# A long-convolution and GLU kernel on one core: six PSUM banks for the transforms and two for the GLU, with a new written order

## The chip, the core and the metric

The kernel runs on one core of a Trainium2 chip. TensorE multiplies matrices and writes its results to PSUM, which has eight banks of 2 KB in each of 128 partitions. VectorE (DVE) and ScalarE (ACT) read PSUM and SBUF. SyncE (SP) issues almost all DMAs here, in one queue. The metric is the time of one execution in device microseconds (us); lower is better. A profile of one execution, taken on the chip, gives the start and duration of every instruction and who waited for whom.

## The reference

Two branches work on the layer-normalised input and are added to it. All tensors are bf16; S is 2048, D is 640, F is 1728.

```python
x = A_q
xn = layernorm(x)                                    # over D
# branch A: a causal convolution over the whole sequence
k_shift = sum over t in 0..3 of k delayed by t, times shift_k[:, t]
kv = k_shift * v
y = irfft(rfft(kv, 2S) * rfft(ssm_k, 2S))[:S]        # per channel, along S
A = xn * (y + kv * ssm_D)
# branch B: a gated linear unit
B = (sigmoid(xn @ w_gate) * (xn @ w_up)) @ w_down
out = x + A + B
```

## The kernel before

The kernel interleaves the two branches on TensorE.

**Branch B** goes in four passes (`tr` 0 to 3) of 512 tokens. A pass transposes its normalised tokens to `xnT` (by TensorE for the first two passes in `rec_tp`, L700; by a transposing DMA for the others, L694). Then it goes through 14 chunks of 128 of F (`rec_fc`, L752): five matmuls for the gate and five for the up projection (L764), each into a PSUM bank of its own; a sigmoid of the gate on ACT (L728 or L722); and a multiply of sigmoid and up on VectorE into `hT` (L730), or, for some chunks, a copy of up to SBUF first (L316) and a multiply from there (L725). The last chunk holds gate and up in one bank. The first two chunks of the first pass are computed in pieces of 128 tokens as they arrive (`rec_first`, L735, matmuls L744). At the end of a pass `rec_down` (L771) projects each of its four 128-token tiles back to 640 columns: 14 chunks for each of two column halves of 320 (L782), and VectorE adds each half to the accumulator `acc` (L794).

**Branch A** treats the 640 channels as two halves of five sub-blocks, ten in all. For each sub-block VectorE makes `kv` from `k` and `v` (`rec_kv`, L468 to L484, eight operations), and TensorE goes through three transform stages: `rec_st1` (L503, once for the kernel spectrum and once for `kv`), `rec_st2` (L523, four groups) and, after a complex product on VectorE (`rec_prod`, L553 and L556, or L547 where a DMA swaps the halves), `rec_st3` (L575 and L577, two groups). Each group of matmuls fills one pair of PSUM banks (stage 1 fills two pairs) and is evacuated by a copy of 1024 elements per partition on ACT (L316, L319) or VectorE (L317, L320). After five sub-blocks `rec_st4` (L607) finishes a half. Stages 1, 2 and 4 use parts of the array (32 or 64 rows); stage 3, the GLU and the down projections use all of it. Before all of that come the fix-up of `k`'s first rows (`load_kv`, L426, with its evacuation L317 or L316) and the shift filter's broadcast (L389).

**What sets the order.** Every operation is recorded with what it reads and writes, and then issued in the order of a written-out list, `ORDER` (L80); the cost figures passed to `pe`, `act` and `dve` and the priorities don't take part in that. An operation that ACT or VectorE could do goes to VectorE if it is in `ON_DVE` (L124). Each engine and SP's queue work in that order. Buffers come from pools named in `SLOTS` (L279): `"c"` are pairs of PSUM banks (two, so four banks), for the transforms, the shift and fix-up matmuls and the first pass's transposes; `"g"` are single banks (four) for GLU and down projections, the second pass's transposes and a warm-up. Where an operation takes a buffer, it gets, among those whose users have all been issued, the one used least recently; on the chip it then waits until those users are done.

The statistics of a token tile (L641 sums, L647 squares) run on ACT, in two batches: tiles 4 to 7 in the first pass, 8 to 15 around the first down projections. Normalised tokens are also written to DRAM (L687).

Of the kernel before, what the change touches and what calls it, by code (L numbers as in the profile page):

```python
# [21 lines left out]
P = 128  # L22
# [20 lines left out]
def _dft_tables():  # L43
# [37 lines left out]
    6, 0, 5, 1, 4, 2, 8, 7, 3, 11, 10, 13, 12, 9, 14, 16, 71, 72, 15, 73, 74, 75, 91, 17, 86, 76, 96, 77, 104, 97,  # L81
    78, 571, 81, 79, 87, 88, 82, 80, 83, 92, 89, 84, 90, 148, 85, 94, 93, 572, 98, 100, 99, 102, 101, 149, 103, 589,
    42, 150, 151, 152, 155, 153, 57, 154, 157, 563, 156, 158, 564, 64, 565, 590, 567, 566, 568, 569, 62, 573, 570,
    18, 61, 574, 575, 63, 577, 58, 576, 578, 579, 56, 581, 580, 582, 59, 583, 585, 107, 584, 106, 586, 607, 587, 108,
    591, 588, 66, 105, 592, 593, 608, 109, 110, 595, 594, 19, 111, 609, 596, 113, 43, 68, 597, 599, 60, 112, 598, 29,
    600, 601, 114, 603, 65, 604, 605, 602, 610, 67, 606, 611, 612, 39, 614, 613, 44, 615, 45, 133, 134, 20, 136, 616,
    617, 23, 619, 135, 618, 27, 620, 621, 116, 623, 31, 622, 625, 624, 118, 626, 115, 32, 627, 41, 120, 628, 119, 40,
    631, 122, 25, 629, 632, 121, 630, 35, 117, 633, 123, 634, 126, 637, 128, 635, 30, 636, 130, 638, 127, 639, 131,
    26, 640, 129, 37, 643, 642, 125, 641, 649, 124, 650, 132, 24, 651, 38, 653, 644, 655, 652, 21, 654, 162, 22, 69,
    645, 656, 646, 657, 658, 36, 647, 648, 33, 659, 660, 34, 163, 662, 95, 164, 165, 663, 664, 172, 167, 667, 665,  # L90
    137, 28, 661, 159, 666, 669, 166, 668, 161, 168, 47, 671, 160, 670, 50, 169, 672, 673, 48, 171, 143, 170, 46,
    178, 674, 144, 52, 173, 676, 180, 54, 179, 677, 138, 49, 174, 678, 51, 181, 175, 139, 680, 53, 675, 183, 182,
    290, 681, 682, 70, 176, 140, 195, 186, 685, 683, 141, 295, 196, 294, 199, 142, 177, 201, 200, 185, 686, 184, 202,
    145, 197, 293, 187, 689, 296, 198, 679, 291, 188, 687, 690, 292, 203, 297, 204, 192, 692, 189, 694, 205, 193,
    206, 695, 194, 207, 190, 209, 208, 191, 227, 210, 217, 228, 216, 233, 146, 234, 219, 211, 147, 218, 231, 220,
    212, 688, 232, 221, 229, 698, 298, 55, 230, 222, 684, 691, 223, 213, 696, 235, 699, 214, 249, 703, 236, 215, 237,
    701, 224, 238, 248, 704, 226, 240, 251, 225, 243, 239, 250, 259, 244, 697, 735, 260, 253, 265, 736, 693, 707,
    700, 252, 705, 266, 241, 755, 706, 711, 242, 702, 254, 261, 708, 263, 255, 262, 712, 280, 709, 264, 713, 267,
    245, 268, 717, 281, 246, 247, 714, 269, 718, 270, 283, 256, 715, 716, 719, 271, 257, 258, 723, 282, 272, 273,
    310, 274, 710, 720, 311, 275, 722, 721, 314, 276, 729, 315, 316, 299, 286, 312, 317, 730, 288, 313, 731, 318,  # L100
    277, 319, 287, 724, 278, 320, 732, 279, 321, 284, 322, 725, 285, 391, 734, 307, 301, 395, 300, 726, 309, 733,
    756, 737, 333, 308, 302, 324, 727, 739, 728, 394, 342, 323, 325, 738, 304, 397, 343, 303, 396, 344, 740, 346,
    392, 305, 345, 393, 332, 741, 347, 348, 743, 326, 349, 289, 742, 327, 350, 351, 746, 744, 374, 352, 367, 745,
    328, 748, 354, 747, 330, 329, 750, 353, 306, 388, 752, 775, 355, 751, 390, 331, 757, 749, 389, 334, 753, 358,
    336, 759, 356, 335, 359, 398, 754, 758, 337, 357, 338, 761, 760, 400, 368, 763, 401, 762, 399, 403, 369, 404,
    764, 766, 765, 371, 370, 767, 768, 372, 375, 769, 776, 770, 373, 381, 376, 772, 795, 771, 378, 797, 377, 777,
    773, 379, 339, 830, 779, 774, 380, 778, 341, 340, 360, 781, 402, 382, 783, 780, 782, 405, 406, 383, 784, 407,
    786, 384, 433, 385, 432, 411, 788, 785, 787, 435, 412, 386, 417, 436, 415, 418, 387, 790, 416, 413, 792, 789,
    791, 414, 796, 798, 419, 793, 420, 794, 361, 800, 362, 799, 363, 364, 365, 802, 801, 806, 803, 805, 422, 421,
    408, 424, 807, 423, 409, 434, 808, 410, 804, 425, 437, 366, 443, 426, 812, 438, 444, 439, 449, 465, 427, 450,  # L110
    464, 813, 467, 428, 468, 445, 447, 446, 809, 448, 814, 831, 810, 429, 811, 451, 815, 430, 431, 452, 818, 817,
# [10 lines left out]
    940, 941, 913, 923, 943, 947, 914, 946, 915, 945, 944, 917, 916, 936, 938, 939, 937  # L122
]
ON_DVE = [  # L124
    45, 133, 135, 620, 622, 34, 144, 179, 183, 141, 196, 145, 146, 266, 247, 258, 315, 329, 773, 340, 416, 364, 448,
    431, 463, 474, 500, 480, 478, 502, 495, 498, 490, 514, 534, 545, 546, 888, 553, 559
]

# [91 lines left out]
def kernel(  # L220
# [107 lines left out]
    def mm(n):  # L328
        return n / 2.4 + 3.0
# [405 lines left out]
    def rec_first(pri):  # L735
# [13 lines left out]
        for fc in range(2):  # L749
            rec_evac(0, fc, cs[fc], gt())  # L750
# [173 lines left out]
```

## Time and profile before

| | us |
|---|---|
| median of 10 runs (lowest to highest) | 270.58 (269.28 to 271.89) |
| profiled execution | 270.83 |
| span in its profile | 269.1 |
| TensorE busy | 256.4 |
| VectorE busy | 189.3 |
| ScalarE busy | 158.2 |
| GLU matmuls (L764), 520 of 128x512 | 121.1 busy |
| down matmuls (L782), 448 of 128x320 | 67.0 busy |

The span is from the first to the last instruction in the profile; the rest of the execution's time lies around it. Matmuls overlap, so the mean duration of one (380 ns for L764) is longer than the distance between two starts (216 ns), and "busy" says little of what is lost. The kernel has one stream of work on TensorE, so what costs time is a stretch in which TensorE works on nothing, or at a lower clock, and the question for each is what it waited for. The page gives the clock that TensorE was granted in tenths of full speed, for 40 slices of 6.7 us.

### The profile page before, as it was taken

The page shows a single profiled execution, that of the slowest core. Times are in us where ns is not written, and L with a number is a line of the kernel's source. Part 1 is how long each engine was busy: PE and PEld are TensorE (multiplying, and loading weights), DVE is VectorE, ACT ScalarE, POOL GpSimd, SP SyncE. Part 2 cuts the span into 40 slices and gives each one's busy share as a digit, 9 for nine tenths or more (in the row PEclk, how much of TensorE's full clock was granted, in tenths as well). Part 3 has the DMA queues.
Part 4 walks back from the last instruction along what each step waited for, and adds up shares of the span by engine and source line. Part 5 has one row for each costly group of instructions (what it writes and reads, how often), then busy time and mean ns, then how long its engine had stood idle before and what let it go on. Part 6 is the DMA issues. An engine that isn't in the chain of part 4 may idle for free.

```text
span 269.1 us, 9709 instructions
## 1 busy us (share of the span) xinstructions
PE 256.4 (95%) x4375; PEld 156.1 (58%) x4375; DVE 189.3 (70%) x329; ACT 158.2 (59%) x235; POOL 0.7 (0%) x6
## 2 busy tenths in 40 slices
PE   8899988999999797999999999999999999999992
PEld 3754435755445555777655546577676466545771
DVE  4433376256999999876979969698776846558541
ACT  3844949962887696646788456556366666422200
POOL 1000000000000000000000000000000000000000
PEclk9999997999999999999999999999999999999998
DMA  6999899999946191999976163371354647400761
GB/s 176 330 327 316 158 216 149 148 138 303 131 104 152 40 298 61 148 158 154 192 148 170 44 185 90 80 174 31 82 146 148 178 94 217 118 2 5 178 178 40
DMA packets 90448, 40.40 MB, mean 150 GB/s; under 512 B 66592, under 2 KB 88040, under 8 KB 90088
## 3 DMA queue, kind: packets, MB, share of 16 engines
q1 hardware_dynamic: 90216, 39.47, 66.8%
q8 instruction: 34, 0.56, 0.9%
q10 hardware_dynamic: 192, 0.33, 0.4%
q14 instruction: 6, 0.05, 0.1%
HBM read 30.61 MB, written 5.24 MB: 133 GB/s over the span
## 4 chain that ended last, share of the span: by engine, by line
PE 76%; DVE 14%; DMA 3%; SPq 2%; ACT 2%; issue 1%; ACTq 1%; DVEq 0%
PE g L764 33%; PE g L782 23%; PE c L523 6%; PE c L607 4%; PE c L575 3%; PE c L577 3%; PE c L503 2%; DVE P L553 2%; DVE ta L473 2%; DVE tb L468 1%; SPq L445 1%; DMA acc<-in_A_q_dram 1%; PE g L744 1%; DMA ht<-in_A_ssm_k_dram 1%; DVE S L556 1%; DVE xq L678 1%
## 5 line engine op out<-in xcount | busy, mean ns | idle before, releaser
L764 PE MATMUL g<-xnT,w 128*128 128x512 bf16 x380 | 89.6, 380 | 0.0
L782 PE MATMUL g<-wd,hT 128*128 128x320 bf16 x448 | 67.0, 304 | 0.0
L764 PEld LDWEIGHTS <-w 128*128 128x128 bf16 x380 | 34.0, 98 | 36.5
L782 PEld LDWEIGHTS <-hT 128*128 128x128 bf16 x448 | 42.8, 99 | 17.8
L730 DVE TENSOR_TENSOR hT<-sig,g 128x512 bf16<-128x512 bf16 x34 | 23.1, 686 | 19.5 <-PE g L764 12.9
L316 ACT CAST S<-c 128x1024 bf16<-128x1024 f32 x31 | 30.8, 1017 | 8.6 <-PE c L523 8.5
L728 ACT ACTIVATE sig<-g 128x512 bf16<-128x512 f32 x34 | 20.2, 596 | 20.0 <-PE g L764 16.9
L764 PE MATMUL g<-xnT,V 128*128 128x512 bf16 x140 | 31.5, 380 | 0.0
L523 PEld LDWEIGHTS <-Mt 64*128 64x128 f16 x1280 | 20.4, 95 | 10.2 <-issue 9.5
L794 DVE TENSOR_TENSOR acc<-g,acc 128x320 bf16<-128x320 f32 x32 | 14.4, 486 | 16.3 <-PE g L782 16.3
L523 PE MATMUL c<-T,Mt 64*128 64x64 bf16 x1280 | 23.9, 191 | 1.7 <-ACT V L316 1.6
L316 ACT CAST V<-c 128x1024 bf16<-128x1024 f32 x17 | 17.0, 1014 | 10.2 <-PE c L577 10.2
L764 PEld LDWEIGHTS <-V 128*128 128x128 bf16 x140 | 13.4, 98 | 15.2
L575 PE MATMUL c<-At,S 128*128 128x128 f16 x160 | 19.8, 220 | 2.2 <-DVE S L556 1.9
L722 ACT ACTIVATE sig<-g 128x512 bf16<-128x512 f32 x18 | 10.8, 602 | 16.5 <-PE g L764 16.2
L316 ACT CAST T<-c 128x1024 bf16<-128x1024 f32 x15 | 14.7, 1015 | 9.6 <-PE c L503 9.4
L577 PE MATMUL c<-At,P 128*128 128x128 f16 x160 | 19.6, 219 | 0.0
L575 PEld LDWEIGHTS <-S 128*128 128x128 bf16 x160 | 15.5, 98 | 4.4 <-DVE S L556 3.6
L319 ACT ACTIVATE T<-c 128x1024 bf16<-128x1024 f32 x14 | 13.9, 1024 | 5.6 <-PE c L503 5.6
L553 DVE TENSOR_TENSOR P<-S 64x1024 bf16<-64x1024 bf16 x20 | 13.7, 685 | 4.6 <-ACT S L316 4.2
L577 PEld LDWEIGHTS <-P 128*128 128x128 bf16 x160 | 15.6, 98 | 1.2 <-issue 0.7
L317 DVE CAST S<-c 128x1024 bf16<-128x1024 f32 x9 | 11.0, 1224 | 4.3 <-PE c L523 4.3
(84 smaller groups left out, 264.5 us busy)
## 6 DMA issues: line engine op xcount, KB each, us to landing
w<-in_B_w_gate_dram SPq DMA_DIRECT2D x7, 640.0 KB, 5.7
w<-in_B_w_up_dram SPq DMA_DIRECT2D x7, 640.0 KB, 5.3
kt<-in_A_k_dram SPq DMA_DIRECT2D x8, 320.0 KB, 7.8
vt<-in_A_v_dram SPq DMA_DIRECT2D x8, 320.0 KB, 5.5
xnd<-xq SPq DMA_DIRECT2D x4, 640.0 KB, 5.2
P<-S SPq DMA_DIRECT2D x10, 256.0 KB, 3.9
ht<-in_A_ssm_k_dram SPq DMA_DIRECT2D x16, 96.0 KB, 4.3
wd<-in_B_w_down_dram SPq DMA_DIRECT2D x3, 480.0 KB, 9.1
```

The costliest lines, as they stand in the source:

```text
L316: fa = lambda: nc.scalar.copy(out=out_fn(), in_=in_fn())
L317: fd = lambda: nc.vector.tensor_copy(out_fn(), in_fn())
L319: fa = lambda: nc.scalar.activation(out_fn(), in_fn(), ACT.Copy, scale=scale)
L523: nc.tensor.matmul(tl[c][:, b, 64 * kk:64 * kk + 64], lhsT=Mb[rows, k, 64 - 64 * r:192 - 64 * r], rhs=tl[T][rows, 2 * k + r].rearrange("p ...
L553: dve(n, 2, lambda a=a, o=o, b=b: nc.vector.tensor_tensor(Q(b)[a], X(b)[a], H(b)[o], ALU.mult), r=sr + ([(Z, b, 1)] if h else []), w=[(Z, ...
L575: nc.tensor.matmul(o, lhsT=tl[S_][:, b, 0, j, :], rhs=Ab[:, 2 if zc else 0, :], start=True, stop=zc)
L577: nc.tensor.matmul(o, lhsT=tl[Z][:, b, j, :], rhs=Ab[:, 1, :], start=False, stop=True)
L728: act(512, lambda: nc.scalar.activation(tl[sg][:], tl[cs[0]][:], ACT.Sigmoid), r=[(cs[0],)], w=[(sg,)], alloc=[(sg, "sig")], pri=pri - 2000)
L730: dve(512, 1, lambda: nc.vector.tensor_tensor(hT[:, fc, :], tl[sg][:], tl[cs[1]][:], ALU.mult), r=[(cs[1],), (sg,)], w=[(hk, fc)], pri=pri ...
L764: nc.tensor.matmul(tl[c][:], lhsT=w()[:, k, o:o + P], rhs=tl[X][:, k, :], start=(k == 0), stop=(k == NC - 1))
L782: nc.tensor.matmul(tl[pd[i]][:, 0:320], lhsT=hT[:, fc, t4 * P:(t4 + 1) * P], rhs=wd[:, fc, 320 * i:320 * i + 320], start=(fc == 0), stop=( ...
L794: dve(320, 1, lambda i=i, m=m, pd=pd: nc.vector.tensor_tensor(acc[:, m, 320 * i:320 * i + 320], tl[pd[i]][:, 0:320], acc[:, m, 320 * i:320 ...
```

## The change

- `SLOTS`: `"c"` has three pairs of banks, and `"g"` two banks; still eight in all.
- `rec_first` and `rec_evac`: the first two chunks of the first pass, gate and up, now go to a pair of banks each from `"c"` (`c0_0`, `c0_1`), not to four banks from `"g"`.
- `rec_down`: every token tile is computed as the last one was before: first column half (chunks 0 to 6, then 7 to 13), then the other half, where a tile's two halves went chunk by chunk together. A half takes its bank when it begins.
- The key `"last"` puts the down projection of token tile 15 behind that of tile 14; before, tile 15 came first and tile 14 ended the kernel.
- `ORDER` and `ON_DVE` are new lists. The shift matmul (operations 42 to 45) comes earlier and so do the copies of `M` (40, 41); the `k` multiplies begin during the first pass's down projections; `ON_DVE` has 30 entries, before 40.
- The cost figures in `pe`, `MG` and `MD` are changed.

```diff
 ORDER = [
...
 ]
 ON_DVE = [
-    45, 133, 135, 620, 622, 34, 144, 179, 183, 141, 196, 145, 146, 266, 247, 258, 315, 329, 773, 340, 416, 364, 448,
-    431, 463, 474, 500, 480, 478, 502, 495, 498, 490, 514, 534, 545, 546, 888, 553, 559
+    45, 136, 135, 622, 34, 160, 182, 141, 140, 145, 202, 215, 210, 264, 313, 308, 330, 285, 371, 378, 384, 431, 450,
+    480, 495, 497, 504, 520, 545, 560
 ]
...
-             "ta": 1, "tb": 1, "T": 2, "S": 2, "P2": 1, "V": 1, "c": 2, "g": 4}
+             "ta": 1, "tb": 1, "T": 2, "S": 2, "P2": 1, "V": 1, "c": 3, "g": 2}
...
     def rec_evac(tr, fc, cs, pri):
+        two = isinstance(cs, str)
+        pk = lambda i: (cs, i) if two else (cs[i],)
+        pv = lambda i: tl[cs][:, i] if two else tl[cs[i]][:]
...
-            act(512, lambda: nc.scalar.activation(tl[sg][:], tl[cs[0]][:], ACT.Sigmoid),
-                r=[(cs[0],)], w=[(sg,)], alloc=[(sg, "sig")], pri=pri - 2000)
-            dve(512, 1, lambda: nc.vector.tensor_tensor(hT[:, fc, :], tl[sg][:], tl[cs[1]][:], ALU.mult),
-                r=[(cs[1],), (sg,)], w=[(hk, fc)], pri=pri - 2000)
+            act(512, lambda: nc.scalar.activation(tl[sg][:], pv(0), ACT.Sigmoid),
+                r=[pk(0)], w=[(sg,)], alloc=[(sg, "sig")], pri=pri - 2000)
+            dve(512, 1, lambda: nc.vector.tensor_tensor(hT[:, fc, :], tl[sg][:], pv(1), ALU.mult),
+                r=[pk(1), (sg,)], w=[(hk, fc)], pri=pri - 2000)
...
     def rec_first(pri):
-        cs = [[f"pg0_{fc}_{u}" for u in range(2)] for fc in range(2)]
-        every = [(cs[fc][u], fc, u) for fc in range(2) for u in range(2)]
+        every = [(fc, u) for fc in range(2) for u in range(2)]
...
-                            nc.tensor.matmul(tl[c][:, i * P:(i + 1) * P], lhsT=weight(0, u)[1]()[:, k, o:o + P],
+                            nc.tensor.matmul(tl[f"c0_{fc}"][:, u, i * P:(i + 1) * P], lhsT=weight(0, u)[1]()[:, k, o:o + P],
...
-                   alloc=[(c, "g") for c, _, _ in grp] if i == 0 else (), pri=FIX + 1)
+                   alloc=[(f"c0_{fc}", "c") for fc in range(2)] if i == 0 else (), pri=FIX + 1)
...
         for t4 in range(4):
...
-            last = m == NQ - 1
-            parts = ([(0, 7, (0,)), (7, 14, (0,)), (0, 7, (1,)), (7, 14, (1,))] if last else
-                     [(c0, c1, (0, 1)) for c0, c1 in ((0, 4), (4, 8), (8, 11), (11, 14))])
+            parts = [(0, 7, (0,)), (7, 14, (0,)), (0, 7, (1,)), (7, 14, (1,))]
...
-                          ([("z",)] if c1 == 14 else []) + ([("cv", u) for u in range(4)] if m >= PRM["ML"] and c0 == 0 else []),
-                          w=[(pd[i],) for i in ii], pri=gt())
+                          ([("z",)] if c1 == 14 else []) + ([("cv", u) for u in range(4)] if m >= PRM["ML"] and c0 == 0 else []) + ([("last",)] if m == NQ - 1 and c0 == 0 else []),
+                          w=[(pd[i],) for i in ii] + ([("last",)] if m == NQ - 2 and c1 == 14 else []), pri=gt())
```

## The prediction

> **What bounds the kernel now.** I read the page's busy shares first, then its slices, the stages by window, and last the chain and the single queues.
>
> ```profile
> PE 256.4 (95%) x4375; PEld 156.1 (58%) x4375; DVE 189.3 (70%) x329; ACT 158.2 (59%) x235; POOL 0.7 (0%) x6
> ...
> PEclk9999997999999999999999999999999999999998
> ```
>
> TensorE is the bound over the whole span, but "busy" covers lost time, so I ask where. One clock digit is a 7, in the slice 40.4 to 47.1 us. The stages by window (columns: stretch, length, busy time of PE, weight loads, DVE, ACT, POOL, clock, DMA share, GB/s):
>
> ```profile
> 38.00:47.00 9.00, 7.26 (x50) 4.41 (x48) 5.81 (x9) 7.68 (x16) 0.00 (x0) 0.81 1.19 174
> 80.00:104.00 24.00, 20.61 (x447) 12.71 (x446) 23.65 (x40) 17.50 (x21) 0.00 (x0) 1.00 0.56 158
> ```
>
> From 80 to 104 us VectorE is busy for 23.65 of 24 us: here it sets the pace, not TensorE. From 38 to 47 us the clock was 0.81. The timeline of that stretch:
>
> ```profile
> 38.97 0.43 PE L389 MATMUL c<-xq,Ft 128*128 128x320 bf16 x2
> ...
> 40.68 0.73 PE L700 MATMUL g<-ident,xq 128*128 128x128 bf16 x10 [1.27 <-DVE xq L678]
> ...
> 42.56 4.71 PE L782 MATMUL g<-wd,hT 128*128 128x320 bf16 x22
> ```
>
> After the first GLU pass TensorE waits for a normalised token tile (1.27 here, 0.47 at the next pair), and 22 down matmuls then take 4.71 us, where the chain has 76 in 10.45 (137 ns each). The trace's clock record is 0.5 from 42.32 for 3.41 us: 1.7 us lost. Now the chain, at a place without gaps:
>
> ```profile
> 163.93 1.19 PE g L764 x5
> 165.12 0.57 PE c L523 x32
> 165.69 1.18 PE g L764 x5
> 166.87 1.04 PE c L523 x64
> ...
> 226.16 7.55 PE g L764 x35
> ```
>
> 35 GLU matmuls in a row are 1.08 us per five; ahead of a transform, five take 1.18 to 1.19. One transform group of L523 is 0.57, two are 1.04, so the second adds 0.47. **Each passage between full-array matmuls (L764, L782, L575/577) and part-array ones (L503, L523, L607) costs 0.10 us**, in either direction: a switch. Adding TensorE's issue times from its first transpose (5.64) to its end (264.21): 258.6 us, of which about 244.3 is work with its switches and 14.3 is waiting: 2.9 at the start, 2.2 around the transposes, 1.7 clock, 5.6 in the convolution's start (75 to 104), and small ones.
>
> **The change, part by part.** All amounts are against the profiled execution: 270.83 us, span 269.1, so 1.7 lie around the span. The median of the runs shown is 270.58, 0.25 below it.
>
> *Banks and order, switches.* With three pairs of banks for transforms, the written order puts more of them side by side. Counted in the order of TensorE's instructions, passages into part-array work fall from 61 to 53, and so do those out of it: 16 x 0.10 = -1.6. But 9 passages between different part-array kinds are new (stage 2 to stages 1 or 4; before there was none), a pair the trace does not show. Bounds: nothing, as between two L523 groups, or a whole switch each, +0.9. I take half: **-1.1** (-1.6 to -0.7).
>
> *Column halves.* 448 down matmuls with 448 weight loads before and after. The last token tile already runs in halves: seven in 0.95 us, 136 ns, as with both columns. Cost 0. A half needs one bank, and its accumulate (L794, 0.49 us) has 0.95 us of cover by the next seven.
>
> *First chunks in the transform banks.* They hold two of three pairs from the start, so the third transpose (psT0_1) waits for the evacuation of psT0_0, 0.69 on ACT; before it had its own pair. Walked from 9.49: **+0.5** (0 to 0.7).
>
> *Two GLU banks.* This is the price. Between the last matmul into a GLU bank and the first of its next user lay at least 3.1 us of TensorE work in 80% of cases before (median 4.2); in the new order the median is 1.8, and 51 of 139 lie under 1.2. A gate bank needs 0.2 to the sigmoid, 0.60 for it and 0.05 back: 0.85. An up bank needs 0.27 + 0.69 + 0.05: 1.01. The dense cover is 1.08, so alone it just fits. It fails where ACT has a queue. In the first pass the statistics of tiles 4 to 7 stand between the sigmoids:
>
> ```profile
> 26.62 0.58 ACT L728 ACTIVATE sig<-g 128x512 bf16<-128x512 f32 x1
> 27.10 0.72 ACT L641 ACTIVATE jk<-acc 128x640 bf16<-128x640 bf16 x1
> ...
> 27.95 0.74 ACT L641 ACTIVATE jk<-acc 128x640 bf16<-128x640 bf16 x1
> ...
> 29.39 0.83 ACT L647 ACTIVATE jk<-acc,st 128x640 bf16<-128x640 bf16 x1
> ...
> 30.34 0.83 ACT L647 ACTIVATE jk<-acc,st 128x640 bf16<-128x640 bf16 x1
> ```
>
> Starts lie 0.86 apart for a sum and 0.95 for a square, 0.48 for a sigmoid. In the new order three sums stand ahead of chunk 7's sigmoid, one sum and a square ahead of chunk 8's, two squares ahead of 9's and one ahead of 10's. By those steps gate matmuls 8, 9, 10 come 0.44, 0.34, 0.21 late. Up matmul 11 takes the bank its own gate has just left, which costs 0.85. Sum **+1.85** (0.8 to 3). Before, four banks hid this. The statistics wait for the DMA of tiles 4 to 7, one large tile load later in SP's queue but one down-weight load earlier: no change taken, up to +1 if late.
>
> *Around the transposes.* The shift matmul and the normalisation now come earlier, so nothing waits for L678. But four transposes share two banks: the second waits for sigmoid and copy on ACT (1.2), the fourth for its predecessor's copy (0.65). End of GLU to first down matmul: 2.9 us, before 42.56 - 38.97 - 0.27 = 3.3: **-0.4**.
>
> *Clock.* TensorE: Matmul & The Clock Gate, "Why this matters for your kernels", says to keep idle gaps under about 3 us. The row disagrees: the longest gap here was 1.27 to 1.6 us and the clock still fell, in a window of which only 0.3 us was matmuls other than transposes (the same page's Part 4 says that transposes don't count as busy in the same way). By gap length the new order is safe; by that reading a stretch of 2.9 us with transposes alone can still trip it, if a 3.41 us window falls on it. The page's "psum-queue depth-cycling" speaks against the whole change: small idles between bank turns lower the clock again and again, each worth 1.7 us here. The row for 80 to 104 us has 3.4 idle us in 24 at clock 1.00, so I take no such fall. By the rule it would be several times +1.7. Taken: **-1.7** (0 if it falls again).
>
> *Convolution's start.* VectorE's work from the halo fix-up of k to the products of the second and third sub-block, by its starts (0.60 for L468/L473, 0.71 for L553, 1.14 for a PSUM cast) against TensorE's work to the same matmul: before, VectorE needs 3.9 us more than TensorE, and the waits came to 5.6. After, the k multiplies start during the down projections (the second near 57.5, before 65.5; VectorE idled 3 us at a time there), with fewer GLU chunks of TensorE's work behind them: the excess is 1.5, and 0.7 go by between k's fix-up matmul and that multiply. With a little idle time I take waits of 2.5: **-3.1** (-5 to 0). ACT takes seven transform evacuations more over the kernel, and by the same sums has 5 us to spare here at its tightest. SP's queue: the last k load stands 43rd, before 41st, with one v load fewer ahead; by the landings of before, k is in near 55 and the down weights at 43 to 44.5, about when they are used. The transpose load of tile group 2 now stands ahead of the second k half, whose four parts then land near 127, when its fix-up is due: 0, up to +2.
>
> *Rest.* In the later stages waits were 0.8. The new order has 14 bank turns under 1.3 us there, where a single VectorE operation of 0.6 in front makes one late: **+1.0** (0 to 5). *Last tile last:* one L794 after the last matmul and not two: **-0.4**.
>
> Sum: -1.1 + 0.5 + 1.85 - 0.4 - 1.7 - 3.1 + 1.0 - 0.4 = -3.35, so 267.5 against the profiled execution. Against the median it would be 267.2; but the clock's fall need not be in each of the runs shown, so part of its 1.7 may not be there to win. **Predicted 267.4 us.**
>
> **The rivals.** (1) *The clock falls again* at the transposes: -1.7 goes, 269.1. For it the gap of 2.9 us; against it, a window must fall just on it. (2) *Two banks become the bound.* Place: GLU passes 2 to 4, where sigmoids and multiplies queue behind VectorE and ACT work. Some 24 turns under 1.3 us from the second pass on; one 0.6 us operation in front costs about 0.4 beyond the slack. From 0.18 us a turn (4.4 us in all) the gain is gone; with two in three late, 16 x 0.4 = 6.4 instead of 1.0, 272.9: slower than before. Against it: VectorE is busy 70%. (3) *VectorE still sets the convolution's start*: its work is nearly the same, and if idle time in its queue eats the early start, -3.1 goes: 270.5, no change. (4) *The squeeze is better hidden*: no waits for ACT in the first pass and none later, 1.85 + 1.0 less: 264.6.
>
> **How the numbers follow.** The main case 0.50 (265.7 to 268.8), clock 0.17, two banks 0.09, VectorE 0.09, better 0.15. A change under 0.3% (0.8 us) cannot be told from none here. Faster takes the main case, the better one, and nearly all of the clock's: 0.83; same 0.09; slower 0.08. The range 264.0 to 270.6 leaves out two banks and the ends of the better case.
>
> **What would show it.** Right: five-matmul groups ahead of transforms fewer; clock digit 9 in the seventh slice; first down matmul near 44.5 instead of 42.6, yet the second GLU pass no later than 0.5 us; waits of L764 for ACT sigmoids of 0.2 to 0.9 near 28 to 37; VectorE's k multiplies from 57; 75 to 104 us with PE busy above 22 of 24. Wrong: a second 0.5 in the clock, waits for L730 spread over 110 to 240 us, or a convolution's start with as much waiting as now.

## The result, and the profile after

The changed kernel takes 268.51 us (median of 14 runs, 267.49 to 270.3), the kernel before 270.39 us beside it (49 runs, 269.28 to 272.05). The ratio is 0.993, with a 95% interval of 0.991 to 0.994. Ratios here are of fast runs alone; of the experiments' runs one counts as slow, at over 1.5% above the fastest of its kernel (a_pairs2, 270.04 us). The forecast was 267.4: the sign was right and the time lies inside the range, but the gain is 1.9 us, not the 3.0 to 3.35 us of the sum. The profiled execution took 269.15 us with a span of 267.4 (before 270.83 and 269.1).

The page after, busy shares and clock:

```profile
PE 254.2 (95%) x4375; PEld 155.8 (58%) x4375; DVE 181.4 (68%) x319; ACT 166.2 (62%) x245; POOL 0.7 (0%) x6
...
PEclk9999999999999999999999999999999999999999
```

No slice of the clock has a digit below 9. The two stretches that the forecast looked at (stretch, length, busy time of PE, weight loads, DVE, ACT, POOL, clock, DMA share, GB/s):

```profile
38.00:47.00 9.00, 6.50 (x49) 3.90 (x48) 4.83 (x8) 5.74 (x10) 0.00 (x0) 1.00 1.02 192
80.00:104.00 24.00, 24.00 (x553) 14.23 (x545) 23.49 (x38) 22.33 (x29) 0.00 (x0) 1.00 0.55 151
```

From 80 to 104 us TensorE now works without a break (24.00; before 20.61), though VectorE is as full as before. From 38 to 47 us it works less than before (6.50; 7.26), at full clock. The timeline of TensorE shows where it waits there (start, length, engine, line, operands, count, idle time ahead and what ended it):

```profile
36.88 1.24 PE L766 MATMUL g<-xnT,w 128*128 128x512 bf16 x5 [0.68 <-ACT sig L731]
...
39.00 3.40 PE L766 MATMUL g<-xnT,w 128*128 128x512 bf16 x15 [0.89 <-DVE hT L733]
...
43.80 0.72 PE L700 MATMUL g<-ident,xq 128*128 128x128 bf16 x10 [1.11 <-ACT xnT L316]
...
45.01 0.44 PE L700 MATMUL g<-ident,xq 128*128 128x128 bf16 x5 [0.50 <-ACT xnT L316]
...
45.29 1.93 PE L782 MATMUL g<-wd,hT 128*128 128x320 bf16 x13
```

The transposes wait in the two places, and for nearly the times, of the forecast (the matmuls that follow are 1.28 and 0.67 us late; forecast 1.2 and 0.65), and the first down matmul starts at 45.29 (forecast near 44.5). But the GLU waits ahead of them are not where the walk put them: gate matmuls 8 to 10 are late by 0.6 us in all (forecast 0.99), up 11 by 0.85 as forecast, and gate 12 by 1.05, where the forecast had nothing. VectorE tells why:

```profile
34.40 0.95 DVE L402 COPY Mt<-Mt 64x3072 f16<-64x3072 f16 x1 [0.73 <-DMA Mt<-dftM]
35.38 0.17 DVE L662 TENSOR_SCALAR st<-st 128x4 f32<-128x4 f32 x1
...
37.77 0.16 DVE L669 SCALAR_TENSOR_TENSOR st<-st 128x4 f32<-128x4 f32 x1
38.26 0.69 DVE L733 TENSOR_TENSOR hT<-sig,g 128x512 bf16<-128x512 bf16 x1 [0.33 <-PE g L766]
```

The multiply that frees up 10's bank (the L733 at 38.26) stands behind the copy of `M`, which waits for its DMA, and behind 13 small operations. The forecast walked ACT's queue and left VectorE's out.

Of the 1.05 us, 0.7 belong to this one execution, in which `M` landed late. Five traces with the same first pass (a_pairs, a_act, a_klate, a_pairs2 and best3 of the experiments) have it in time. In a_pairs VectorE and TensorE go on like this:

```profile
33.65 0.95 DVE L402 COPY Mt<-Mt 64x3072 f16<-64x3072 f16 x1
...
38.24 3.40 PE L766 MATMUL g<-xnT,w 128*128 128x512 bf16 x15 [0.41 <-DVE hT L733]
```

The copy doesn't wait, gate 12 is late by 0.35 us, and from the shift matmul to the first transpose it is 13.9 us in all five, where the profiled execution of the changed kernel has 14.6.

The pair of kinds that the trace before could not show, and an old one:

```profile
102.07 1.11 PE L523 MATMUL c<-T,Mt 64*128 64x64 bf16 x64
103.11 1.25 PE L766 MATMUL g<-xnT,w 128*128 128x512 bf16 x5
...
152.38 0.64 PE L523 MATMUL c<-T,Mt 64*128 64x64 bf16 x32
152.95 0.69 PE L607 MATMUL c<-V,Bt 32*32 32x80 bf16 x64
```

A group of stage 2 ahead of stage 4 takes 0.57 us from start to start; between two groups of stage 2 it takes 0.475 (the 1.04 from 102.07 to 103.11 are two groups and one switch). So the passage from one part-array kind to another costs a whole switch of 0.10, not half of one.

At the end one accumulate follows the last matmul instead of two; from TensorE's end to the end of the span it is 4.3 us (before 4.9):

```profile
263.10 0.49 DVE L794 TENSOR_TENSOR acc<-g,acc 128x320 bf16<-128x320 f32 x1 [1.41 <-PE g L782]
```

The sum of the forecast against TensorE's issue times in the two traces. The last row was not in the forecast:

| term | forecast, us | the two traces, us |
|---|---|---|
| switches | -1.1 | -0.7 |
| first chunks in the transform banks | +0.5 | +0.4 |
| two GLU banks, first pass | +1.85 | +2.5 (0.7 of it the late `M`) |
| around the transposes | -0.4 | -0.3 |
| clock | -1.7 | -1.55 |
| convolution's start (50 to 120 us) | -3.1 | -2.0 (waits 5.5 before, 3.5 after) |
| rest | +1.0 | +0.4 |
| end | -0.4 | -0.55 |
| first transpose starts later | | +0.2 |
| sum | -3.35 | -1.6 (spans: -1.7) |

Each trace is one execution, and runs of one kernel spread over 2 to 3 us, so a term is good to a few tenths. The clock's row needs the experiments: it is right for these two executions and wrong for the kernel.

### The profile page after: what moved, and what is told of

The parts are those of the page before. It is cut to its first block, busy times and chain, and to the rows that moved or that the text cites. A ratio compares the mean times of both kernels' runs of the same rounds, so it can differ in the third digit from the quotient of the medians.

```text
span 267.4 us, 9723 instructions
## 1 busy us (share of the span) xinstructions
PE 254.2 (95%) x4375; PEld 155.8 (58%) x4375; DVE 181.4 (68%) x319; ACT 166.2 (62%) x245; POOL 0.7 (0%) x6
## 4 chain that ended last, share of the span: by engine, by line
PE 64%; DVE 22%; DMA 5%; issue 3%; ACT 3%; SPq 0%; DVEq 0%; ACTq 0%
PE g L766 26%; PE g L782 21%; PE c L523 5%; DVE P L553 4%; DVE ta L473 4%; PE c L607 4%; DVE tb L468 3%; DMA V<-in_B_w_up_dram 2%; PE c L575 2%; PE c L577 2%; DVE hT L733 2%; PE c L503 2%; DMA ht<-in_A_ssm_k_dram 2%; PE c L746 2%; DVE S L556 2%
## 5 line engine op out<-in xcount | busy, mean ns | idle before, releaser
L782 PE MATMUL g<-wd,hT 128*128 128x320 bf16 x448 | 64.9, 300 | 0.0
L316 ACT CAST S<-c 128x1024 bf16<-128x1024 f32 x33 | 32.7, 1020 | 16.0 <-PE c L523 15.9
L733 DVE TENSOR_TENSOR hT<-sig,g 128x512 bf16<-128x512 bf16 x32 | 21.9, 685 | 17.6 <-PE g L766 12.3
L794 DVE TENSOR_TENSOR acc<-g,acc 128x320 bf16<-128x320 f32 x32 | 15.6, 489 | 24.1 <-PE g L782 23.9
L731 ACT ACTIVATE sig<-g 128x512 bf16<-128x512 f32 x32 | 19.2, 600 | 18.8 <-PE g L766 15.0
L316 ACT CAST V<-c 128x1024 bf16<-128x1024 f32 x19 | 18.6, 1014 | 7.9 <-PE c L577 7.8
L316 ACT CAST T<-c 128x1024 bf16<-128x1024 f32 x18 | 17.6, 1023 | 3.2 <-PE c L503 3.1
L725 ACT ACTIVATE sig<-g 128x512 bf16<-128x512 f32 x18 | 10.8, 603 | 10.9 <-PE g L766 9.9
L319 ACT ACTIVATE T<-c 128x1024 bf16<-128x1024 f32 x14 | 13.9, 1025 | 3.9 <-PE c L503 3.9
L728 DVE TENSOR_TENSOR hT<-sig,hT 128x512 bf16<-128x512 bf16 x18 | 7.6, 426 | 12.6 <-ACT hT L316 12.5
```

The costliest lines, as they stand in the source:

```text
L316: fa = lambda: nc.scalar.copy(out=out_fn(), in_=in_fn())
L319: fa = lambda: nc.scalar.activation(out_fn(), in_fn(), ACT.Copy, scale=scale)
L725: act(512, lambda: nc.scalar.activation(tl[sg][:], pv(0), ACT.Sigmoid), r=[pk(0)], w=[(sg,)], alloc=[(sg, "sig")], pri=pri - 2000)
L731: act(512, lambda: nc.scalar.activation(tl[sg][:], pv(0), ACT.Sigmoid), r=[pk(0)], w=[(sg,)], alloc=[(sg, "sig")], pri=pri - 2000)
L733: dve(512, 1, lambda: nc.vector.tensor_tensor(hT[:, fc, :], tl[sg][:], pv(1), ALU.mult), r=[pk(1), (sg,)], w=[(hk, fc)], pri=pri - 2000)
L782: nc.tensor.matmul(tl[pd[i]][:, 0:320], lhsT=hT[:, fc, t4 * P:(t4 + 1) * P], rhs=wd[:, fc, 320 * i:320 * i + 320], start=(fc == 0), stop=( ...
```

## The experiments

Names with a_ start from the changed kernel, names with b_ from the kernel before; best1 to best3 build on a_pairs2. Each ratio is to the kernel before on the same chip, with its 95% interval; the changed kernel stands at 0.993 (0.991 to 0.994).

### The clock: the idle time filled with matmuls, and with transposes

b_fill_mm, in the transposes of token tile group 1:

```diff
+        def fill(n):
+            for _ in range(n):
+                nc.tensor.matmul(tl['c_fill'][:, 0, :], lhsT=ident[:], rhs=hT[:, 0, :], start=True, stop=True)
         def tp(i, o):
+            if tr == 1 and i in (0, 2):
+                fill(5 if i == 0 else 2)
```

> The kernel before, with seven more matmuls of 512 columns that nobody reads (five ahead of the first transpose of token tile group 1, two ahead of its third), written to a pair of transform banks that is free; they fill idle time of 1.27 and 0.47 us while TensorE waits for the normalised tiles. Theory A (the clock falls because its window holds next to no matmuls other than transposes): the clock stays at 1.0, 22 down matmuls take 3.0 us and not 4.7, and the time falls by about 1.6 us, to some 268.8, from which follows that -1.7 of the forecast's sum was right in size. Rival B (the fall has another cause, or the time is given back while VectorE sets the pace): 0 within 0.4 us.

> The kernel before, with the same two idle times filled by 20 and 8 transposes of the identity, of 128 columns each, in place of matmuls; about 1.1 and 0.45 us as well. Theory A (transposes don't count as busy for the clock): the clock falls to 0.5 as in the kernel before, and the time stays at 270.4 within 0.4 us. Rival B (the length of the gap decides, whatever fills it): no fall, and the time drops by 1.6 us as with matmuls.

Measured: with matmuls 271.12 us, ratio 1.0015 (1.000 to 1.003); with transposes 274.24 us, ratio 1.012 (1.009 to 1.016). The timeline of TensorE with matmuls as filling:

```profile
39.59 1.24 PE L700 MATMUL c<-hT,ident 128*128 128x512 bf16 x5
41.02 0.73 PE L706 MATMUL g<-ident,xq 128*128 128x128 bf16 x10 [0.19 <-DVE xq L678]
...
42.79 7.50 PE L788 MATMUL g<-wd,hT 128*128 128x320 bf16 x54
```

The filling works: 54 down matmuls take 7.5 us, 139 ns each, and the clock stays at 1.0. Yet no time is won. The mean clock is on record for each run. Of the 86 runs of the kernel before that stand beside the experiments, 15 have a mean clock of 0.991 or less, and their median is 271.6 us; the other 71 have at least 0.995, and a median of 270.4 us. So the fall costs about 1.2 us where it happens, but it happens in about one run of six, and the profiled execution was one of these. Its absence is worth 0.2 us of the mean and 0.1 of the median. With matmuls as filling none of 22 runs has such a clock, on a chip where the kernel before has it in 8 of 27; with transposes none of 6, which says little. Rival B of the first expectation is right about the time, for a reason that neither named. On transposes theory A is not confirmed, and what trips the clock stays open.

The traces hint at why it is a matter of chance. Every stretch between two changes of the clock is a multiple of 3.413 us (before the fall 37.55, which is 11 of them, after it 221.87, which is 65; in b_early 259.41, which is 76), and these steps lie elsewhere in each trace: the record begins 4.77 us from the start in the trace before and 6.85 in b_early's. Whether the stretch with little work falls into one step may then decide. No run tests this.

In b_fill_mm's trace TensorE waits 0.6 us for a sigmoid at 58.05, where the trace before has no wait (b_early's has one of 0.5), and the waits of the convolution's start stay at 5.5. Why the filled kernel is 0.6 us slower than the 19 runs without a fall on the same chip (median 270.5 us) is not explained. The transposes lost 3.3 us far from their place, which is told in the last section.

### The first pass: VectorE's order

a_first, in the written order (602: multiply 10, 606: multiply 11, 40 and 41: the copies of `M`, 114: the small operations):

```diff
-    ... 58, 41, 600, 601, 114, 609, 603, 29, 605, 604, 602, 133, 136, ...
+    ... 58, 600, 601, 602, 114, 609, 603, 29, 605, 604, 606, 133, 136, ...
```

> The changed kernel, with three moves on VectorE in the first GLU pass: chunk 10's multiply goes ahead of the first half of the M copy and of the 13 small operations of the reciprocal square root (L662 to L669), chunk 11's multiply goes behind these, and both halves of the M copy go behind the transposes' copies, where VectorE idles. Up matmul 11 then gets a bank of its own. Theory A (the waits of the first pass are on the path that sets the end): the waits of 0.85 us ahead of up 11 and of 1.05 us ahead of gate 12 go, one of about 0.9 us ahead of up 12 comes in their place, because chunk 11's multiply stands behind the 2.6 us of small operations; the time falls by about 1.0 us against the changed kernel (some 267.5 by its median). Rival B (VectorE sets the start of the convolution, whose work can't start before k has landed near 54 us): TensorE's first pass ends 1.0 us earlier, but the waits between 56 and 115 us grow by as much, and the time stays within 0.3 us of the changed kernel's 268.5.

Measured: 268.98 us, ratio 0.9925 (0.990 to 0.995): not to be told from the changed kernel. The trace: up 11 waits no more, but up 12 comes 0.83 us late for multiply 11, and chunk 13 comes 0.56 us late for a sigmoid that two normalisations precede on ACT. From the shift matmul to the first transpose it is 14.1 us. That is less than the 14.6 us of the changed kernel's own trace, but 0.2 more than in the five traces whose `M` landed in time: the two new waits are 0.2 us longer than the two that went. So nothing was won in the first pass, and the run can't tell theory A from rival B.

### The transposes: a wait that a free bank alone doesn't remove

a_pairs, the allocation, and a_pairs2, the order in addition (617, 619, 621, 623: the transposes; 615, 616: chunk 13's sigmoid and multiply; the others: copies):

```diff
-            p_ = f"pst{tr}_{i}" if not fast else f"psT{tr}_{i // 2}"
+            p_ = f"psT{tr}_{i // 2}"
...
-            al = [] if fast and i % 2 else [(p_, "c" if fast else "g")]
+            al = [] if i % 2 else [(p_, "c")]
```

```diff
-    614, 613, 67, 617, 615, 30, 618, 616, 619, 621, 620, 622, 623, ...
+    614, 613, 67, 617, 619, 621, 623, 615, 616, 618, 620, 622, 624, 30, ...
```

> The changed kernel, with token tile group 1's four transposes in two of the three pairs of banks, which are free then, and no longer in the two GLU banks. Theory A: the waits of 1.28 and 0.67 us between the transposes go, the first down matmul starts near 43.4 us and not 45.3 (the down weights land at 43.0 and 43.3), and the time falls by about 1.9 us, to some 266.6. Rival B (VectorE sets the start of the convolution): the down projections start 1.9 us earlier, but the k multiplies don't, and the time falls by less than 0.7 us.

> The changed kernel, with token tile group 1's four transposes in two pairs of transform banks, as in the run before (a_pairs), and now also ordered so that all four stand ahead of the first copy out of them: in that run the second transpose of a pair still waited for the copy of the first (1.11 us), since both use one tile. Theory A (this wait is on the path that sets the end): no wait between the transposes, first down matmul at about 43.3 us where it was at 45.3 (the down weights land at 43.0 and 43.3), the time 1.5 to 1.9 us below the changed kernel's 268.5. Rival B (VectorE and the landing of k, near 54 us, set the start of the convolution): the down projections start 1.9 us earlier, the waits from 56 to 115 us grow from 3.5 to more than 5, and the time stays within 0.4 us.

Measured: a_pairs 268.70 us, ratio 0.992 (0.989 to 0.995), no gain; a_pairs2 266.95 us, ratio 0.985 (0.982 to 0.988), under the changed kernel by 1.6 us in the medians and by 2.1 us in the ratios. Of its four runs three took 265.8 to 266.98 us and one 270.04, at a mean clock of 0.994. The two in TensorE's timeline, first a_pairs:

```profile
41.48 0.44 PE L700 MATMUL c<-ident,xq 128*128 128x128 bf16 x5
43.03 0.72 PE L700 MATMUL c<-ident,xq 128*128 128x128 bf16 x10 [1.11 <-ACT xnT L316]
44.33 0.44 PE L700 MATMUL c<-ident,xq 128*128 128x128 bf16 x5 [0.58 <-DVE xnT L317]
```

then a_pairs2:

```profile
41.48 1.28 PE L699 MATMUL c<-ident,xq 128*128 128x128 bf16 x20
42.59 7.63 PE L781 MATMUL g<-wd,hT 128*128 128x320 bf16 x55
```

In a_pairs the banks are free, but the copy of the first transpose is written ahead of the second one into the same tile, and the wait stays. With all four transposes ahead of the copies the down projections start 2.0 us earlier than in a_pairs, and all of it reaches the end (from the first transpose to TensorE's end 255.05 us, in a_pairs 257.0): theory A. These waits ahead of the second pass are on the path; the convolution's start does not swallow them. This kernel has the lowest median and the lowest ratio of all that were run.

### The convolution's start: VectorE relieved, k late, k early

a_act gives two copies to ACT:

```diff
 ON_DVE = [
-    45, 136, 135, 622, 34, 160, 182, 141, 140, ...
+    45, 136, 135, 622, 34, 141, 140, ...
```

> The changed kernel, with two copies of 1.13 us out of the transform banks (stage 1 of the first two sub-blocks, on VectorE at 59.4 and 62.9 us) given to ACT, which idles for 6 of the 19 us from 56 to 75. Theory A (VectorE sets the pace from 57 to 114 us, so whatever is taken off it there moves the convolution's start): the waits of 0.41 and 0.55 us at the start of the second GLU pass go, those of 0.24, 0.31, 0.94 and 0.50 us between 103 and 115 shrink, and the time falls by 1.5 to 2.5 us, to some 266.5. Rival B (ACT is as full as VectorE from 75 to 104 us, 27.3 of 29, and sets the pace with it): less than 0.7 us.

Measured: 268.76 us, ratio 0.994 (0.991 to 0.996). Nothing is won. TensorE's timeline in a_act, at the waits that were to shrink (in the changed kernel 0.76 at 110.12 and 0.33 at 114.97):

```profile
108.80 1.11 PE L523 MATMUL c<-T,Mt 64*128 64x64 bf16 x64 [0.77 <-DVE S L317]
...
113.65 0.23 PE L575 MATMUL c<-At,S 128*128 128x128 f16 x1 [0.33 <-DVE S L556]
```

They are the same to 0.01 us after 2.3 us of VectorE's work have gone. They are not a backlog that VectorE carries along from 57 us, as the forecast's sums took it. At the second pass's start the waits only changed their owner (0.59 and 0.25 us, with ACT's sigmoid behind two more copies, for 0.41 and 0.55).

a_klate delays six k operations in the changed kernel:

```diff
-    643, 162, 37, 642, 124, 33, 644, 28, 34, 131, 163, 159, 647, ... 164, 38, 649, 165, 172, 181, 651, 167, ... 132, ...
+    643, 37, 642, 124, 33, 644, 28, 34, 131, 159, 647, ... 38, 649, 181, 651, ... 132, 162, 163, 164, 165, 172, 167, ...
```

> The changed kernel, with the first six multiplies and adds of k (from 55.4 us on) moved on VectorE behind the accumulates of the down projections, the first multiply of the second GLU pass and the small operations of the second reciprocal square root, so that they begin near 64 us, as in the kernel before (60.4 and 65.5). Nothing else is moved: banks, TensorE's order and ACT's order stay. Theory A (the early k multiplies are what shortens the convolution's start): VectorE idles about 3 us more between 55 and 62, the waits of TensorE between 75 and 120 grow from 2.2 us to 4 to 5.5, those of 0.41 and 0.55 at the second pass's start go, and the time rises by 1 to 2.5 us, to 269.5 to 271. Rival B (three pairs of banks are what shortens it, by letting transforms stand side by side): within 0.5 us of 268.5.

b_early hastens them in the kernel before:

```diff
-    643, 642, 125, 641, 649, 124, 650, 132, ... 654, 162, ... 648, 33, 659, 660, 34, 163, 662, 95, 164, 165, ... 172, 167, ...
+    643, 33, 642, 125, 641, 162, 34, 163, 164, 165, 172, 167, 649, 124, 650, 132, ...
```

> The kernel before, with its four GLU banks, two pairs and its own order of TensorE, but for one matmul: the k fix-up (L426) is issued during the last tile's down projection, and on VectorE the first six multiplies and adds of k stand right behind it, ahead of the second reciprocal square root, as the change has them (they begin near 56 us, not at 60.4 and 65.5). Theory A (the early k multiplies alone shorten the convolution's start): the 5.5 us of TensorE's waits from 80 to 104 us fall to 2 to 3.5 and the time falls by 2 to 3 us, to about 268. Rival B (they need the changed banks and order of transforms, too): the multiplies come early, VectorE then idles for the bank turns of stages 1 and 2, the waits stay above 5 us, and the time stays within 0.5 us of 270.5.

Measured: a_klate 273.17 us, ratio 1.009 (1.006 to 1.011), 4.3 us above the changed kernel; b_early 270.62 us, ratio 1.000 (0.999 to 1.002). Both expectations for a_klate miss: the time lies above the range of either. TensorE loses it at once, in the second pass, and not from 75 us on, as was expected:

```profile
72.59 4.42 PE L765 MATMUL g<-xnT,V 128*128 128x512 bf16 x10 [3.39 <-DVE hT L732]
```

A GLU chunk's multiply stands behind the late k operations, and with two GLU banks the next chunk has no bank; the clock falls there too (0.5 from 71.34 us for 6.83), so part of the 4.3 us is the clock's (its two runs with a mean clock of 0.997 and more took 271.7 and 272.8 us). In b_early VectorE's timeline shows the early work, and what it comes to:

```profile
55.17 0.68 DVE L467 TENSOR_TENSOR ta<-kt,sT 128x1024 bf16<-128x1024 bf16 x1
...
58.62 0.68 DVE L472 TENSOR_TENSOR ta<-ta,kvt 128x1024 bf16<-128x1024 bf16 x1
...
65.30 0.69 DVE L729 TENSOR_TENSOR hT<-sig,g 128x512 bf16<-128x512 bf16 x1 [1.26 <-PE g L763]
68.00 0.43 DVE L724 TENSOR_TENSOR hT<-sig,hT 128x512 bf16<-128x512 bf16 x1 [2.02 <-ACT hT L315]
```

The six operations end at 59.3 us, 9 us earlier than before, and then VectorE stands idle for GLU chunks: 1.26 us until TensorE has computed one, 2.02 us until ACT has copied the up half of another. From 75 us on everything is as before, with 5.5 us of waits. So the early k operations alone bring nothing; in the new order the work that follows depends on them.

What the waits of the convolution's start were for, the trace before tells:

```profile
91.39 0.64 PE L523 MATMUL c<-T,Mt 64*128 64x64 bf16 x32 [0.53 <-ACT V L316]
...
102.37 0.23 PE L575 MATMUL c<-At,S 128*128 128x128 f16 x1 [1.16 <-DVE S L556]
```

The second is a wait for data, VectorE's product. The first is not: stage 2 doesn't read `V`, and ACT's copy of it frees a pair of banks. Five of the eight waits from 75 to 105 us, 2.7 us of their 5.25, end with such a copy on ACT out of a transform bank, and they stand in b_early's trace as well. In the changed kernel no wait of TensorE from 75 to 115 us ends with ACT; those left there end with VectorE. This fits the third pair of banks as what shortened the convolution's start, rival B of b_early. It is not shown by a run: two pairs and four GLU banks were not tried with the new order.

### Column halves alone

b_halves, in `rec_down`, with three operations (652, 712, 807) moved behind what they now need:

```diff
-            parts = ([(0, 7, (0,)), (7, 14, (0,)), (0, 7, (1,)), (7, 14, (1,))] if last else
-                     [(c0, c1, (0, 1)) for c0, c1 in ((0, 4), (4, 8), (8, 11), (11, 14))])
+            parts = [(0, 7, (0,)), (7, 14, (0,)), (0, 7, (1,)), (7, 14, (1,))]
```

> The kernel before, with the down projections of all token tiles by column halves (seven chunks, then seven, first for one column half, then for the other) in the same four places of the order; three operations go a few places later, since their data now come later (the second pass's first multiply, and the first halves of the last chunk's users in two groups). The last token tile stays last but one. Theory A: seven matmuls of one column half take 0.95 us as before, so nothing in the passes; after the last matmul only one L794 of 0.49 us is left and not two (the second starts 0.41 us after the first): the time falls by 0.4 us, which 5 rounds can hardly tell from none. Rival B: halves bind a bank longer or later, so that waits appear among the downs: 0.5 to 1.5 us slower.

Measured: 270.57 us, ratio 1.0005 (0.999 to 1.002). Halves cost nothing that the runs can tell (-0.3 to +0.6 us), as forecast. The trace has two waits among the down projections that the trace before has not, 0.42 us at 109.08 and 0.68 at 178.54, each for a GLU chunk's multiply, as rival B said; the changed kernel's trace has neither. The 0.4 us at the end could not show: the written order of the kernel before keeps both of tile 14's accumulates behind its last matmul, and they follow it here too (0.89 us for the two).

### Together

best1: a_pairs2, a_act, and the first pass's small operations in two parts around multiply 10. best2: the same without a_act, the load of `M` behind the last down weights, three VectorE operations earlier at the second pass's start. best3: a_pairs2, these three moves, and four of ACT's sums on VectorE. The order in best2, apart from what a_pairs2 has and from the moves in the first pass:

```diff
-    ... 19, 584, 106, 39, 586, ... 60, 46, ... 649, 165, 172, 181, 651, 167, ... 182, 650, ... 648, ... 652, ... 140, ... 670, ...
+    ... 19, 584, 106, 586, ... 60, 39, 46, ... 649, 165, 648, 172, 181, 651, 167, ... 650, 652, 182, ... 670, 140, ...
```

> Everything together: a_pairs2, a_act, and the first pass's VectorE order mended further than in a_first: the reciprocal square root's first six small operations stand ahead of chunk 10's multiply and its last seven behind it, chunk 11's multiply follows them, one normalisation on ACT goes behind chunk 12's sigmoid, the M copies go behind the transposes. Theory A (the waits add up): the first pass loses about 1.9 us of its 2.2 us of waits, the transposes 1.9 (less where the down weights, which land near 42, come later than the transposes), VectorE's part 1.5 to 2.5; in all 264.0 to 265.5 us. Rival B (k, which lands at 52 to 54 us, and VectorE after it set the convolution's start): only VectorE's part is won, and the time is 266.5 or more.

> a_pairs2 with further moves, none of them onto ACT: the first pass's VectorE order of best1; the load of the M table (768 KB) goes in SP's queue behind the last down weights, so that these no longer land at 42 to 43 us; at the second pass's start the last accumulate of the down projections goes ahead of two k operations and the first multiply ahead of a copy of stage 1, so that up 0 gets a bank of its own; chunk 4's multiply goes ahead of one normalisation. Theory A (each wait is on the path): against a_pairs2 (ratio 0.985, 266.4 us on the scale of 270.5) the first pass loses 1.2 to 1.5 us and the second pass's start 0.8 to 1.3: 263.6 to 264.5 us. Rival B (k, landing at 52 to 54 us whatever the first pass does, and ACT's statistics, which end near 60 us, hold the second pass): the first pass's gain turns into waits between 56 and 75 us, and the time is 265.5 to 266.5.

> a_pairs2, with four of the eight sums of token tiles 8 to 15 computed on VectorE (one reduction each, about 0.75 us) in its idle time among the down projections, and no longer on ACT, whose statistics ran without a break from 46 us until the second GLU pass was due (60.6 us in the changed kernel, about 58.7 in a_pairs2); and with the three VectorE moves of best2 at the second pass's start. Theory A (in best1 and best2 it was ACT's statistics, and the copies and sigmoids queued behind them, that took back what the first pass had won): ACT is free 2.5 to 3 us earlier, the waits of 0.43 and 0.56 us at the second pass's start go, and the time is 0.8 to 1.3 us under a_pairs2 (ratio 0.980 to 0.982, some 265.3 us). Rival B (VectorE's or TensorE's own order holds it, and VectorE now has 3 us more to do): within 0.4 us of a_pairs2 or slower.

Measured: best1 268.02 us, ratio 0.990 (0.987 to 0.993); best2 267.77 us, 0.990 (0.987 to 0.994); best3 267.81 us, 0.990 (0.987 to 0.993). None is shown to be faster than a_pairs2 (and, with overlapping intervals, none to be slower); theory A's sum fails in all three. In the traces a new wait takes back each gain. In best1 it is 13.0 us from the shift matmul to the first transpose, 0.9 less than in a_pairs2, but then:

```profile
42.90 7.37 PE L795 MATMUL g<-wd,hT 128*128 128x320 bf16 x53 [1.46 <-DMA wd<-in_B_w_down_dram]
...
61.01 0.41 PE L505 MATMUL c<-Ft,ht 32*128 32x64 f16 x30 [0.96 <-ACT T L321]
```

TensorE waits for the down weights, and then for ACT, whose statistics run without a break from 45.3 to 60.1 us. This execution also has a fall of the clock (0.5 from 63.16 for 3.41 us, mean 0.994); among the other traces only those of before and a_klate have one while TensorE works:

```profile
PEclk9999999997999999999999999999999999999999
```

With the weights earlier (best2) it is an accumulate behind the copies of `M` (0.67 us), again ACT (0.66), and then VectorE. From the first transpose to TensorE's end best2 takes 255.0 us, as a_pairs2 does, though its first pass is 1.2 us shorter. With ACT relieved (best3) the waits are for the down weights again (0.90) and for VectorE. VectorE's wait in best2 and in best3:

```profile
68.33 1.89 PE L779 MATMUL g<-xnT,V 128*128 128x512 bf16 x8 [1.22 <-DVE hT L746]
...
68.91 1.46 PE L767 MATMUL g<-xnT,V 128*128 128x512 bf16 x6 [1.22 <-DVE hT L734]
```

a_pairs2 has no such wait. It is in both kernels that move three VectorE operations earlier at the second pass's start, so it came with these moves and not with ACT's relief, which no run has alone.

## Why the prediction was right or wrong

Right in sign and within the range; 1.1 us too low. Step by step:

- **Clock, -1.7.** The step that failed most. The size was right for the execution profiled (1.55), but the sum was made against one execution and carried over to the median. The forecast said that the fall need not be in each run and took off 0.2 us for it; with one run in six it should have taken off 1.5. That the new order keeps the clock was right: none of the 14 runs after, nor of the 19 of a_first, a_pairs and a_act, has a mean clock under 0.996, even though 3 us with transposes alone are still there.
- **Convolution's start, -3.1.** The end was right (TensorE busy 24.00 of 24 us), the cause was not. The step compared sums of VectorE's and TensorE's work from a point that the early k multiplies had moved. b_early moves it alone and wins nothing; a_act takes 2.3 us off VectorE and the later waits stay. And half of the waits before, 2.7 us, were for ACT to empty one of two pairs of transform banks, a term that the step did not have. The engines do not run free of each other between two points: each chunk's multiply ties VectorE to TensorE, and with two banks TensorE to VectorE. The waits fell by 2.0 us; 1.4 us of those left are new, at the second pass's start, where the forecast's sum has no term.
- **Two GLU banks, first pass, +1.85.** Right in kind, 2.5 in the profiled execution. In the five traces with `M` in time it is 1.8, the forecast's size, but by luck: gates 8 to 10 lost 0.4 us less than walked, and gate 12 lost 0.35 us behind VectorE's queue, which the step didn't walk.
- **Switches, -1.1.** Right for the passages counted; the nine new ones cost a whole switch each, the end of the bounds that the step did not take. So -0.7.
- **First chunks, transposes, column halves, end.** As forecast, within 0.2 us. a_pairs2 adds that the transposes' 2 us were the change's to lose: they sit in the two GLU banks while three pairs stand free.
- **Rest, +1.0.** 0.4: of the 14 short bank turns only one was late in the trace, by 0.24 us (149.05). A stop of 0.76 us at 170.70 is a stage 4 matmul's, labelled issue, and no GLU bank's. The rival of two banks as the bound did not come; the Trainium skill's section "psum-queue depth-cycling" (page TensorE: Matmul & The Clock Gate) was not seen at work, with 1.0 in every slice.

If the fall is worth no more than 0.2 us, the table's other rows would leave next to nothing, where the medians stand 1.9 apart. Traces without the fall close most of this gap. b_early and b_halves take the time of the kernel before, and their clock stayed at 1.0 from 38 to 47 us; a_pairs and a_act take the time of the changed kernel:

| trace | span, us | first transpose at | from it to TensorE's end | waits after 50 us, without 75 to 104 |
|---|---|---|---|---|
| before (with the fall) | 269.1 | 5.64 | 258.6 | 1.1 |
| b_early | 268.5 | 6.28 | 257.4 | 1.9 |
| b_halves | 269.1 | 6.28 | 258.0 | 2.5 |
| after | 267.4 | 5.85 | 257.2 | 4.5 |
| a_pairs | 266.9 | 5.59 | 257.0 | 4.4 |
| a_act | 266.9 | 5.81 | 256.8 | 5.0 |

Without the fall the spans of before are 268.8 in the mean and those of after 267.1: 1.7 apart, 0.55 of it at the end, 0.5 ahead of the first transpose, and 0.7 between. The execution that the forecast was made from had lost 1.55 us to the clock, but was ahead of b_early and b_halves by 0.64 us at the first transpose, and by 0.8 and 1.4 us in small waits after 50 us. So the errors of the sum cancelled: the fall was counted as if it were in every run, and the rest was measured against an execution that was quick elsewhere. From the first of the 12 warm-up matmuls to the first transpose it is 4.4 to 5.1 us in these traces, so its 0.5 us may well be chance; whether the small waits are missing because of the fall, three traces don't tell.

## What to carry to other kernels

A loss that one profiled execution shows is worth its size times how often it happens: look at the clock of every run before counting it as a gain. Where two engines hand each other buffers in a fixed order, taking work off one of them upstream can move idle time and not the end, as in a_act; walk every queue between a buffer's last use and its next, and test by moving the work alone in the old order. And when a wait names a buffer, see whether the bank or the written order holds it: here free banks brought nothing until the four writers stood ahead of the readers, and then 2 us.

## What the runs showed of the hardware

A clock fall with short gaps: the Trainium skill's page TensorE: Matmul & The Clock Gate, "Why this matters for your kernels", speaks of gaps of about 3 us; here the clock fell in 15 of 86 runs of a kernel whose trace, taken from one of these, has no gap over 1.6 us once TensorE is at work, and in none of 22 with the gaps filled by matmuls. The changed kernel, with single gaps of 1.1 us among transposes, did not fall in 14.

TensorE can stop with nothing to wait for. b_fill_tp adds 28 transposes near 40 us; TensorE's waits from 120 us on grow from 1.0 to 5.8 us. One of 1.27 us is for VectorE; three are stops labelled issue inside runs of part-array matmuls, of 0.45, 1.39 and 1.04 us:

```profile
183.52 0.19 PE L523 MATMUL c<-T,Mt 64*128 64x64 bf16 x1 [1.39 <-issue]
```

Issue means that no semaphore and no DMA of data was late. The changed kernel has one such stop (0.57 us at 170.70), the kernel before none; every other trace of the new order has it at the same group of stage 4, at 0.32 to 0.86 us, so it is no chance of one execution. The added instructions shift all that follow in TensorE's program; that their fetching is what stalls is a guess that no run here tests.
